# A new order of scores, sums and feed-forward products in the later blocks of an attention and gated-convolution kernel

## The chip, the cores and the metric

The kernel runs on one core of one Trainium2 chip. The metric is the device time of one execution in microseconds (us); before and after are compared by the median of several runs.

## The reference

Attention with a soft cap, and on its output a gated feed-forward layer whose gate is a causal convolution of five taps:

```python
# q, k, v: (8, 12, 448, 64)
scores = (1.0 / np.sqrt(64)) * np.matmul(q, k.transpose(0, 1, 3, 2))
scores = cap * np.tanh(scores / cap)
attn = np.exp(scores - np.max(scores, axis=-1, keepdims=True))
attn = attn / (np.sum(attn, axis=-1, keepdims=True) + 1e-09)
x = np.matmul(attn, v)           # heads side by side: (8, 448, 768)
# xp is x with 4 rows of zeros ahead; conv_w: (5, 768); w_val, w_out: (768, 768)
gate_pre = sum(conv_w[k] * xp[:, k:k + 448, :] for k in range(5))
gate = 1.0 / (1.0 + np.exp(-gate_pre))
out = (gate * (x @ w_val)) @ w_out
```

## The kernel before

The work is cut into 48 head pairs p (8 batches of 6 pairs, two heads side by side on the 128 partitions). For a pair, q and k are loaded in blocks and transposed on VectorE (`tq`, `tk`; lines L296). From pair 13 (`NPLAIN`) on they are split into a high and a low half (`half_hi` on ScalarE, L302, `half_lo` on VectorE, L236) and a score tile is the sum of three products of halves, for both heads: `scores`, L317, tile `pss`, i = 0 to 3 for the four tiles of 112 keys; there are two `pss` buffers. ScalarE makes tanh (L325) and exp (L329) of a tile into `pt`. VectorE adds the four exp tiles of a pair up in `add` (i = 0 and 1: two tiles each, L339; i = 2: the two results, L336). TensorE multiplies them with v (`attnv`, L354, tile `psa`) and with ones (`sums`, L366, tile `psz`). VectorE turns the sums (L374), takes the reciprocal (L380, L381), spreads it (L387) and multiplies (`norm_mul`, L395) into `u`, the pair's 128 columns of x. x is split again: `x_hi` on ScalarE (L400), `x_lo` on VectorE (L236). `conv` has five steps on VectorE (i = 0: L414; 1 to 4: L416), each on top of the one before.

The feed-forward layer of a batch works on its six 128-column blocks. `val` (L437 to L439, tile `psf`) is the product with w_val, 18 matmuls in two parts for a block d; `gate` (L443, VectorE) multiplies it with the sigmoid of the convolution (L422, ScalarE, six of them in one pair of each batch, with a table load), `gated_hi` (L446, ScalarE) and `gated_lo` (L236, VectorE) split the result into `g_h` and `g_l`. `out_part` (L466 to L468, tile `psf`) is the product with w_out, again 18 matmuls, over d = 0 to 5 in this order and so with the block of d = 5 in its last three; `store` (L474, ScalarE) copies it out. There are two `psf` buffers.

No scheduler orders the engines. Each step has a time in units of a pair (`STEADY`, `SPLIT` and other tables for the steps of a pair, `VAL`, `SIG_AT`, `OUT_EVEN` and so on for those of a batch), the steps are sorted by pair + time, and each engine works its instructions off in the order in which they were recorded, waiting on semaphores. So av at 1.10 of pair p stands in the next pair's period, between that pair's scores (0.0, 0.05) and its tanh of tiles 2 and 3. In pairs 13 to 47 the order on TensorE within a period is: scores 0 and 1, `attnv` and `sums` of the pair before, a first feed-forward product, scores 2 and 3, a second one (in two pairs of every second batch two at once). Counted within a batch's six pairs, the feed-forward products lag behind: the pairs with p mod 6 = 1 hold the sigmoids and the value products of d = 1 and 2, p mod 6 = 2 those of d = 3 and 4, p mod 6 = 3 the value product of d = 5 and the first output product, the pairs with 4, 5 and 0 output products, and 0 also the value product of d = 0 of the next batch.

Of the kernel before, what the change touches and what calls it, by code (L numbers as in the profile page):

```python
# [91 lines left out]
    "x_lo": 1.46,  # L92
    "conv": (1.44, 1.54, 1.58, 1.70, 1.74),
}

LATE_X = {"x_lo": 1.76, "conv": (1.78, 1.80, 1.83, 1.86, 1.89)}
NEARLY, NPAIRED, NPLAIN = 6, 11, 13
# [100 lines left out]
def fast_path(tc, io, u2, q, k, v, w_val, conv_w, w_out, out, capt):  # L198
# [8 lines left out]
    NPAIR = H // 2  # L207
    NP = B * NPAIR
# [12 lines left out]
    with ExitStack() as ctx:  # L221
# [77 lines left out]
        def half_hi(name, p):  # L299
            st = state[p]  # L300
            st[name, "h"] = scratch["qk"].tile([P, S], F32R, name=name + "h")
            nc.scalar.copy(st[name, "h"], st[name])  # L302

        def half_lo(name, p):
            st = state[p]
            st[name, "l"] = scratch["qk"].tile([P, S], F32R, name=name + "l")
            less(nc.vector, st[name, "l"], st.pop(name), st[name, "h"])
# [175 lines left out]
        tables = [EARLY if p < NEARLY - 1 else HANDED if p < NEARLY else PAIRED if p < NPAIRED else STEADY if p < NPLAIN else SPLIT for p in range(NP)]  # L483
        for p in range(NPLAIN, NP):
            if p % NPAIR == 0:
                tables[p] = tables[p] | LATE_X

        def at(when, f, *a):
            events.append((when, len(events), f, a))

# [5 lines left out]
            q_hi=lambda p: half_hi("q", p), k_hi=lambda p: half_hi("k", p),  # L496
            q_lo=lambda p: half_lo("q", p), k_lo=lambda p: half_lo("k", p),
            scores=scores, tanh=tanh, exp=exp, add=add, av=attnv, sums=sums, turn_sums=turn_sums, recip=norm_recip,
            spread=spread, mul=norm_mul, x_hi=x_hi, x_lo=x_lo, conv=conv,
        )  # L500
        for p, table in enumerate(tables):
            for name, f in steps.items():
                x = table.get(name, ())
                if isinstance(x, tuple):
                    for i, y in enumerate(x):
                        at(p + y, f, p, i)
                else:
                    at(p + x, f, p)
        for b in range(B):
            t0 = NPAIR * b  # L510
            for d in range(NCC):
                sig = SIG_AT if b else SIG_FIRST
                y = (VAL if b else VAL_FIRST)[d]
                at(t0 + sig, sigmoid, b, d)
                for i in range(PARTS):
                    at(t0 + y + i * PART, val, b, d, i)
                done = t0 + max(y + PARTS * PART, sig + 0.17)
                at(done + 0.01, gate, b, d)

                last = d == NCC - 1  # L520
                at(done + (0.02 if last else 0.08), gated_hi, b, d)
                at(done + (0.03 if last else 0.12), gated_lo, b, d)
            if b % 2 == 0:
                at(t0 + KEEP_AT, keep_tail)
            for m, y in enumerate(OUT_ODD if b % 2 else OUT_LATE if b == B - 2 else OUT_EVEN):
                for i in range(PARTS):
                    at(t0 + y + i * PART / 2, out_part, b, m, i)
                at(t0 + y + 0.20, store, b, m)
                at(t0 + y + 0.40, store_out, b, m)
# [137 lines left out]
def kernel(tc, q, k, v, cap, w_val, conv_w, w_out, out):  # L667
    nc = tc.nc
    with tc.tile_pool(name="cap_pool", bufs=1) as pool, tc.tile_pool(name="io", bufs=2) as io:
        capt = pool.tile([P, 1], F32, name="capt")  # L670
        nc.sync.dma_start(capt, cap.rearrange("(o c) -> o c", o=1).partition_broadcast(P))

        pad = conv_w.shape[0] - 1
        u2 = [pool.tile([P, pad + q.shape[2]], F32, name=f"u{i}") for i in range(2)]
        for t, src in zip(u2, (q, k)):
            load_blocks(nc, t[:, pad:], src, 0)
        mag = pool.tile([1, 1], F32, name="mag")
        nc.vector.scalar_tensor_tensor(mag, capt[0:1], -1.0, capt[0:1], ALU.mult, ALU.max)
        small = pool.tile([1, 1], I32, name="small")
        nc.vector.tensor_scalar(small, mag, CAP_FAST, None, ALU.is_le)  # L680
        flag = nc.values_load(small, min_val=0, max_val=1)
        with tc.If(flag != 0) as cmp:
            fast_path(tc, io, u2, q, k, v, w_val, conv_w, w_out, out, capt)
        with cmp.Else():
            general_path(tc, q, k, v, w_val, conv_w, w_out, out, capt)
# [30 lines left out]
```

## Time and profile before

| | us |
|---|---|
| median of 3 runs | 774.95 |
| lowest, highest | 773.33, 777.27 |
| the profiled execution: its time | 775.05 |
| the profiled execution: span from first to last instruction | 773.3 |
| TensorE (PE) busy | 731.7 |
| VectorE (DVE) busy | 594.9 |
| ScalarE (ACT) busy | 538.8 |

The profiled execution took 775.05, of which 773.3 lie between its first and its last instruction; the rest lies around it. Matmul durations overlap each other, since a matmul starts before the one ahead of it has ended, so the starts are what tells TensorE's pace.

### The profile page before, as it was taken

The numbers are of one execution on the slowest core, as the hardware profiler recorded it, in microseconds if no ns is written. First come the engines' busy times: TensorE is split into PE (matmuls) and PEld (weight loads), VectorE is DVE, ScalarE is ACT, GpSimd is POOL, SyncE is SP. The second block draws the span as 40 slices with busy tenths as digits, with TensorE's granted clock in tenths as the row PEclk, the third lists the DMA queues.
The fourth block names the chain that finished last, engine by engine and source line by source line (L and its number), as shares of the span: only waits on it lengthen the run. The fifth ranks groups of instructions, "written<-read, shape, count | busy, mean of one in ns | idle before, by whom it ended". The sixth has DMA issues, their size and how long they took to land.

```text
span 773.3 us, 10851 instructions
## 1 busy us (share of the span) xinstructions
PE 731.7 (95%) x3972; PEld 490.6 (63%) x3972; DVE 594.9 (77%) x972; ACT 538.8 (70%) x708; POOL 7.8 (1%) x16
## 2 busy tenths in 40 slices
PE   5787899999899999999999999999999999999997
PEld 1232356455676776676766777676666777575997
DVE  2688859878888778998898778998798778997510
ACT  4787677866877669767777669767777669766311
POOL 0000000100000000000000000000000000000000
PEclk9999999999999999999999999999999999999999
DMA  6888745484312333233322333234322333210001
GB/s 117 196 205 216 160 102 133 107 225 98 70 36 52 74 81 57 42 70 83 77 43 47 79 75 62 40 68 85 75 48 47 73 73 71 36 36 31 22 21 65
DMA packets 241820, 63.75 MB, mean 82 GB/s; under 512 B 228448, under 2 KB 235616, under 8 KB 241760
## 3 DMA queue, kind: packets, MB, share of 16 engines
q1 hardware_dynamic: 241760, 62.98, 37.1%
q8 instruction: 33, 0.54, 0.3%
q14 instruction: 27, 0.22, 0.1%
HBM read 51.94 MB, written 11.01 MB: 81 GB/s over the span
## 4 chain that ended last, share of the span: by engine, by line
PE 41%; DVE 20%; ACT 13%; issue 3%; DVEq 0%; ACTq 0%
PE psf L466 7%; PE pss L317 7%; PE psf L467 6%; PE psf L468 6%; PE psa L354 6%; DVE pa L339 4%; ACT pt L325 4%; ACT pt L329 4%; DVE gate L416 3%; PE psf L437 3%; PE psf L438 2%; PE psf L439 2%; ACT gate L422 2%; PE psz L366 2%; DVE g_l L236 1%
## 5 line engine op out<-in xcount | busy, mean ns | idle before, releaser
L325 ACT ACTIVATE pt<-pss,rc 112x896 f32<-112x896 f32 x192 | 186.0, 1005 | 35.4 <-PE pss L317 35.4
L329 ACT ACTIVATE pt<-pt,capt 112x896 f32<-112x896 f32 x192 | 189.2, 1038 | 0.1
L354 PE MATMUL psa<-pt,vn 112*64 112x448 f32 x720 | 147.7, 548 | 0.0
L416 DVE SCALAR_TENSOR_TENSOR gate<-u,cw,gate 128x448 f32<-128x448 f32 x192 | 132.3, 689 | 6.6 <-ACT gate L412 1.1
L466 PE MATMUL psf<-wo,g_h 128*128 128x384 f32 x336 | 117.8, 350 | 0.8 <-DVE wo L142 0.8
L437 PE MATMUL psf<-xh,wv 128*128 128x448 f32 x288 | 110.1, 382 | 5.8 <-DVE gate L443 3.1
L467 PE MATMUL psf<-wo,g_h 128*128 128x384 f32 x336 | 113.1, 337 | 1.1 <-DVE wo L146 1.1
L468 PE MATMUL psf<-wo,g_l 128*128 128x384 f32 x336 | 113.2, 337 | 0.0
L438 PE MATMUL psf<-xh,wv 128*128 128x448 f32 x288 | 105.3, 365 | 0.0
L439 PE MATMUL psf<-xl,wv 128*128 128x448 f32 x288 | 105.2, 365 | 0.0
L339 DVE TENSOR_TENSOR pa<-pt 112x896 f32<-112x896 f32 x84 | 91.1, 1084 | 16.1 <-ACT pt L329 16.1
L354 PEld LDWEIGHTS psa<-pt,vn 112*64 112x64 f32 x720 | 47.5, 137 | 82.3 <-issue 73.3
L400 ACT CAST xh<-u 128x448 fp32r<-128x448 f32 x48 | 27.1, 565 | 86.8 <-DVE u L395 86.8
L466 PEld LDWEIGHTS psf<-wo,g_h 128*128 128x128 f32 x336 | 63.5, 189 | 23.1 <-issue 17.8
L437 PEld LDWEIGHTS psf<-xh,wv 128*128 128x128 f32 x288 | 54.5, 189 | 34.0 <-issue 20.9
L374 DVE STREAM_TRANSPOSE zt<-psz 128x448 f32<-128x448 f32 x45 | 29.0, 644 | 60.2 <-PE psz L366 60.1
L317 PE MATMUL pss<-qt,kt 64*112 64x448 f32 x208 | 53.2, 630 | 22.8 <-ACT pt L325 14.2
L467 PEld LDWEIGHTS psf<-wo,g_h 128*128 128x128 f32 x336 | 63.6, 189 | 1.4 <-DVE wo L146 1.4
L468 PEld LDWEIGHTS psf<-wo,g_l 128*128 128x128 f32 x336 | 63.5, 189 | 0.3
L446 ACT CAST g_h<-gate 128x448 fp32r<-128x448 f32 x48 | 26.3, 562 | 48.5 <-DVE gate L443 48.3
L474 ACT COPY osb<-psf 128x384 f32<-128x384 f32 x56 | 26.8, 479 | 45.9 <-PE psf L468 45.9
L317 PE MATMUL pss<-qh,kh 64*112 64x448 f32 x280 | 58.5, 412 | 0.0
(74 smaller groups left out, 904.5 us busy)
## 6 DMA issues: line engine op xcount, KB each, us to landing
vn<-in_v_dram SPq DMA_DIRECT2D x96, 112.0 KB, 2.6
out_dram<-osb SPq DMA_DIRECT2D x56, 192.0 KB, 1.9
qn<-in_q_dram SPq DMA_DIRECT2D x188, 56.0 KB, 2.5
kn<-in_k_dram SPq DMA_DIRECT2D x188, 56.0 KB, 2.4
w_raw<-in_moe_w_val_dram SPq DMA_DIRECT2D x12, 384.0 KB, 4.6
w_late<-in_moe_w_val_dram SPq DMA_DIRECT2D x12, 384.0 KB, 5.1
w_raw<-in_moe_w_out_dram SPq DMA_DIRECT2D x12, 384.0 KB, 3.8
w_late<-in_moe_w_out_dram SPq DMA_DIRECT2D x12, 384.0 KB, 4.4
```

The source lines that it names most:

```text
L317: nc.tensor.matmul(ps[:CH, j, :S], st[x][r, c], st[y][r], start=(n == 0), stop=(n == len(parts) - 1))
L325: nc.scalar.activation(st["p", i], st.pop(("s", i)), AF.Tanh, scale=rc8[:CH])
L329: nc.scalar.activation(t, t, AF.Exp, scale=capt[:CH])
L339: nc.vector.tensor_tensor(st["a", i], st["p", 2 * i], st["p", 2 * i + 1], op=ALU.add)
L354: nc.tensor.matmul(st["o"][r, :S], vloads[p][:, j, i], t[:, j], start=(i == 0), stop=(i == NKT - 1))
L416: nc.vector.scalar_tensor_tensor(g, u[:, i:i + S], cw[:, hp, i:i + 1], g, ALU.mult, ALU.add)
L437: nc.tensor.matmul(o, w_h, xh, start=(c == 0), stop=False)
L438: nc.tensor.matmul(o, w_l, xh, start=False, stop=False)
L439: nc.tensor.matmul(o, w_h, xl, start=False, stop=(c == NCC - 1))
L466: nc.tensor.matmul(o, g_h[:, d, s], w_h, start=(d == 0), stop=False)
L467: nc.tensor.matmul(o, g_h[:, d, s], w_l, start=False, stop=False)
L468: nc.tensor.matmul(o, g_l[:, d, s], w_h, start=False, stop=(d == NCC - 1))
```

## The change

Three new tables are laid over the tables of pairs 14 to 47, except those with p mod 6 = 1, which hold the sigmoids (`together`). In such a pair (`TOGETHER`) scores 2 and 3 move from 0.62 and 0.67 to 0.31 and 0.32, right behind the `sums` of the pair before (0.28) and ahead of the first feed-forward product (0.36); their tanh and exp move up as well, and all three adds are done in the pair itself (0.52, 0.60, 0.61) and not in the next (1.03, 1.06). `NEXT_TOGETHER`, for the pair ahead of such a pair, moves the end of that pair's work, which falls in the next period: convolution steps 1 to 4 go from 1.61 to 1.70 to 2.16 to 2.19, two periods on. `PREPARE_TOGETHER` moves the low halves of q and k of the pair behind such a pair. The work itself, its tiles and its buffers stay as they are.

```diff
--- before.py
+++ after.py
@@ -93,6 +93,19 @@
     "conv": (1.44, 1.54, 1.58, 1.70, 1.74),
 }
 
+
+TOGETHER = {
+    "scores": (0.0, 0.05, 0.31, 0.32),
+    "tanh": (0.06, 0.13, 0.34, 0.36),
+    "exp": (0.22, 0.29, 0.47, 0.53),
+    "add": (0.52, 0.60, 0.61),
+}
+NEXT_TOGETHER = {
+    "turn_sums": 1.41, "recip": 1.42, "spread": 1.43, "mul": 1.44, "x_hi": 1.45, "x_lo": 1.54,
+    "conv": (1.58, 2.16, 2.17, 2.18, 2.19),
+}
+PREPARE_TOGETHER = {"q_hi": -0.69, "k_hi": -0.68, "q_lo": -0.44, "k_lo": -0.43}
+
 LATE_X = {"x_lo": 1.76, "conv": (1.78, 1.80, 1.83, 1.86, 1.89)}
 NEARLY, NPAIRED, NPLAIN = 6, 11, 13
 
@@ -484,6 +497,17 @@
         for p in range(NPLAIN, NP):
             if p % NPAIR == 0:
                 tables[p] = tables[p] | LATE_X
+
+        def together(p):
+            return NPLAIN < p < NP and p % NPAIR != 1
+
+        for p in range(NPLAIN, NP):
+            if together(p - 1):
+                tables[p] = tables[p] | PREPARE_TOGETHER
+            if together(p):
+                tables[p] = tables[p] | TOGETHER
+            if together(p + 1):
+                tables[p] = tables[p] | NEXT_TOGETHER
 
         def at(when, f, *a):
             events.append((when, len(events), f, a))
```

On TensorE, where pair 27 (p mod 6 = 3) has the end of the value product of d = 5 (L437 to L439; psf, xh, xl are its result and the halves of x) and the start of the first output product (L466 to L468; g_h and g_l are the halves of the gated blocks), there stands before:

```order
1086 L437 MATMUL psf<-xh,wv 128x448
1087 L438 MATMUL psf<-xh,wv 128x448
1088 L439 MATMUL psf<-xl,wv 128x448
1089 L317 MATMUL pss<-qh,kh 112x448 x2
1090 L317 MATMUL pss<-ql,kh 112x448 x2
1091 L317 MATMUL pss<-qh,kl 112x448 x2
1092 L317 MATMUL pss<-qh,kh 112x448 x2
1093 L317 MATMUL pss<-ql,kh 112x448 x2
1094 L317 MATMUL pss<-qh,kl 112x448 x2
1095 L466 MATMUL psf<-wo,g_h 128x384
1096 L467 MATMUL psf<-wo,g_h 128x384
1097 L468 MATMUL psf<-wo,g_l 128x384
```

The six rows with pss, scores 2 and 3, lie between the two products. After the change the lines have other numbers (317 is now 330, 437 to 439 are 450 to 452, 466 to 468 are 479 to 481), and the same place, from the end of the value product on, with the waits, is:

```order
1392 L451 MATMUL psf<-xh,wv 128x448
1393 L452 MATMUL psf<-xl,wv 128x448
1394 L479 MATMUL psf<-wo,g_h 128x384 [waits DVE_49,Pool_49]
...
1407 L480 MATMUL psf<-wo,g_h 128x384
1408 L481 MATMUL psf<-wo,g_l 128x384 [waits DVE_49]
1409 L479 MATMUL psf<-wo,g_h 128x384 [waits Activation_49]
1410 L480 MATMUL psf<-wo,g_h 128x384
1411 L481 MATMUL psf<-wo,g_l 128x384 [waits DVE_49]
1412 L330 MATMUL pss<-qh,kh 112x448 [waits PE_49]
```

The output product now follows the value product directly; its last three matmuls, those of d = 5, wait for ScalarE's g_h and VectorE's g_l, and the scores of pair 28 stand behind them.

On VectorE, in the same pair, from the multiplication into u (L395) on, there stands before (pa are the sums of exp tiles, L339 and L336):

```order
477 L395 TENSOR_TENSOR u_63<-psa,zt 128x448
478 L339 TENSOR_TENSOR pa_3742<-pt 112x896
479 L236 TENSOR_TENSOR ql<-qt,qh 128x448
480 L236 TENSOR_TENSOR kl<-kt,kh 128x448
481 L236 TENSOR_TENSOR xl<-u_63,xh 128x448
482 L414 TENSOR_SCALAR gate<-u_63,cw 128x448
483 L416 SCALAR_TENSOR_TENSOR gate<-u_63,cw,gate 128x448
484 L443 TENSOR_TENSOR gate<-psf,gate 128x448
485 L416 SCALAR_TENSOR_TENSOR gate<-u_63,cw,gate 128x448
486 L236 TENSOR_TENSOR g_l<-gate,g_h 128x448
487 L416 SCALAR_TENSOR_TENSOR gate<-u_63,cw,gate 128x448 x2
488 L339 TENSOR_TENSOR pa_3806<-pt 112x896
```

The gate of d = 5 (L443) and its g_l stand between the convolution steps, ahead of the second add. After the change, from the four convolution steps that have come into this period up to the same gate and g_l:

```order
465 L429 SCALAR_TENSOR_TENSOR gate<-u_64,cw,gate 128x448 x4
466 L387 STREAM_TRANSPOSE zt<-psz 128x448
...
470 L408 TENSOR_TENSOR u_63<-psa,zt 128x448
471 L352 TENSOR_TENSOR pa_3761<-pt 112x896
472 L249 TENSOR_TENSOR xl<-u_63,xh 128x448
473 L249 TENSOR_TENSOR ql<-qt,qh 128x448
474 L249 TENSOR_TENSOR kl<-kt,kh 128x448
475 L427 TENSOR_SCALAR gate<-u_63,cw 128x448
476 L352 TENSOR_TENSOR pa_3771<-pt 112x896
477 L349 TENSOR_TENSOR pa_3761<-pa_3761,pa_3771 112x896
478 L456 TENSOR_TENSOR gate<-psf,gate 128x448
479 L249 TENSOR_TENSOR g_l<-gate,g_h 128x448
```

The gate has come to stand behind both adds (L352 with pa_3771 and L349), and four convolution steps of the pair before stand ahead of the turn of the sums (L387).

## Rows read from the trace of the kernel before

**Rows 1.** The page: span, busy times, and the group of convolution steps 1 to 4.

```profile
span 773.3 us, 10851 instructions
PE 731.7 (95%) x3972; PEld 490.6 (63%) x3972; DVE 594.9 (77%) x972; ACT 538.8 (70%) x708; POOL 7.8 (1%) x16
...
L416 DVE SCALAR_TENSOR_TENSOR gate<-u,cw,gate 128x448 f32<-128x448 f32 x192 | 132.3, 689 | 6.6 <-ACT gate L412 1.1
```

**Rows 2.** Timeline of TensorE, pair 29: start, duration, what.

```profile
436.85 0.46 PE L317 MATMUL pss<-qh,kh 64*112 64x448 f32 x2
...
438.26 0.60 PE L354 MATMUL psa<-pt,vn 112*64 112x448 f32 x2
...
441.32 0.92 PE L366 MATMUL psz<-pa,ones 112*64 112x448 f32 x4
442.17 0.45 PE L466 MATMUL psf<-wo,g_h 128*128 128x384 f32 x1
...
445.23 0.34 PE L468 MATMUL psf<-wo,g_l 128*128 128x384 f32 x1
445.50 0.46 PE L317 MATMUL pss<-qh,kh 64*112 64x448 f32 x2
...
446.91 0.44 PE L466 MATMUL psf<-wo,g_h 128*128 128x384 f32 x1
...
453.38 0.46 PE L317 MATMUL pss<-qh,kh 64*112 64x448 f32 x2
```

**Rows 3.** Timeline of TensorE, pair 27 and the start of pair 28.

```profile
405.96 0.46 PE L317 MATMUL pss<-qh,kh 64*112 64x448 f32 x2
...
414.79 0.37 PE L439 MATMUL psf<-xl,wv 128*128 128x448 f32 x1
...
416.50 0.44 PE L466 MATMUL psf<-wo,g_h 128*128 128x384 f32 x1
...
419.58 0.34 PE L468 MATMUL psf<-wo,g_l 128*128 128x384 f32 x1
419.85 0.46 PE L317 MATMUL pss<-qh,kh 64*112 64x448 f32 x2
```

**Rows 4.** Timeline of ScalarE: pair 27, and tanh 0 of pair 29.

```profile
418.19 0.57 ACT L446 CAST g_h<-gate 128x448 fp32r<-128x448 f32 x1 [3.60 <-DVE gate L443]
418.66 1.90 ACT L325 ACTIVATE pt<-pss,rc 112x896 f32<-112x896 f32 x2
...
437.76 1.01 ACT L325 ACTIVATE pt<-pss,rc 112x896 f32<-112x896 f32 x1 [0.32 <-PE pss L317]
```

**Rows 5.** Timeline of TensorE, last pair: v products and sums of pair 47.

```profile
709.30 3.23 PE L354 MATMUL psa<-pt,vn 112*64 112x448 f32 x16
714.24 0.97 PE L366 MATMUL psz<-pa,ones 112*64 112x448 f32 x4 [1.72 <-DVE pa L336]
```

**Rows 6.** Timeline of VectorE, pair 27 and the start of pair 28.

```profile
411.39 0.65 DVE L374 STREAM_TRANSPOSE zt<-psz 128x448 f32<-128x448 f32 x1
...
413.85 1.08 DVE L339 TENSOR_TENSOR pa<-pt 112x896 f32<-112x896 f32 x1
...
416.45 0.45 DVE L414 TENSOR_SCALAR gate<-u,cw 128x448 f32<-128x448 f32 x1
...
417.54 0.62 DVE L443 TENSOR_TENSOR gate<-psf,gate 128x448 f32<-128x448 f32 x1
...
418.79 0.63 DVE L236 TENSOR_TENSOR g_l<-gate,g_h 128x448 fp32r<-128x448 f32 x1
...
422.45 1.09 DVE L339 TENSOR_TENSOR pa<-pt 112x896 f32<-112x896 f32 x1 [1.72 <-ACT pt L329]
423.58 1.09 DVE L336 TENSOR_TENSOR pa<-pa,pa 112x896 f32<-112x896 f32 x1
```

**Rows 7.** Windows: stretch, busy time of each engine (instructions), granted TensorE clock, DMA.

```profile
209.00:215.00 6.00, 4.01 (x15) 3.38 (x12) 5.73 (x10) 4.51 (x6) 0.00 (x0) 0.72 0.08 13
712.00:717.00 5.00, 3.28 (x19) 2.08 (x16) 3.71 (x6) 0.00 (x0) 0.00 (x0) 1.00 0.12 43
```

## The prediction

> **What bounds the kernel now.** I read the page first. The reader is to see that TensorE is busy for 95% of the span, VectorE for 77%, ScalarE for 70% [rows 1]. A busy share says little about slack, so I went on to the timeline of TensorE and walked one head pair after another, each from its first score matmul to that of the next pair (pairs 0 to 47; pair 27 begins at 405.96, pair 29 at 436.85).
>
> Pair 29 shows what a pair costs when nothing waits [rows 2]: two score tiles 1.41 us (436.85 to 438.26), the products with v of the pair before 3.06, its sums 0.85, one output product 3.33, two more score tiles 1.41, then two output products 6.47: 16.53 together. Within a product the 18 matmuls start 0.18 apart (442.17 to 445.23 is 17 steps); from its last matmul to a score it is 0.27. So TensorE runs without a gap, and a change can win only the seams between kinds of work and the few waits left.
>
> The waits: pair 28 has the same work as pair 29 and took 17.00 (419.85 to 436.85), 0.47 more [rows 2, 3]. ScalarE shows why: a cast of a gated block waited 3.60 for VectorE and stood ahead of tanh 2 and 3 of pair 27, which began at 418.66 [rows 4]; everything behind them, the adds on VectorE included, came late, and the sums of pair 27 with them. The other wait is at the end: from the first v product of pair 47 to its sums it is 4.94 (709.30 to 714.24) where pair 29 has 3.06, so 1.88 of waiting for the adds [rows 2, 5].
>
> **What the change removes.** Scores 2 and 3 go behind the sums, so the seam "product, then score" in the middle of a pair turns into "product, then product". That is 0.27 against 0.18, 0.09 saved; I take the same where one product is of w_val. Sums to score I price like sums to product. Of the 34 pairs from 14 on, 29 have the new table, and pair 47 had no first product to be moved past: 28 x 0.09 = 2.6 us. [...]
>
> The 0.47 of each pair that follows the first output product (16, 22, 28, 34, 40, 46) goes, since tanh 2 and 3 now stand far ahead of that cast and both adds are done in the pair itself: 6 x 0.47 = 2.8. For pair 47 I walked VectorE: its two adds can run once exp 3 is done, before its sums are due, so 1.9 goes as well. Pairs 13, 19, 25, ... with sigmoids keep their tables and so does the wait behind them. Gains together 7.3; the seams could give nothing and the tail nothing, so 2.8 to 7.3.
>
> The four late convolution steps of a pair move into the next one, behind the transposes of q and k, where in most pairs VectorE would wait for the sums anyway. ScalarE does the same work in another order and stays below TensorE. DMAs stand in the same order on SP's queue. None of these is on the path, but for one place.
>
> **What it adds.** That place is the pair with the last value product of a block and its first output product (15, 21, 27, 33, 39, 45). The output product needs, for its last three matmuls, the sixth gated block: the value product, then VectorE's gate, ScalarE's cast to g_h, VectorE's g_l. Before, scores 2 and 3 lay between the two products and the gate stood early on VectorE: gate at 417.54, cast 418.19, g_l 418.79 to 419.42 [rows 4, 6]; the last three matmuls of a product that ran from 416.50 to 419.58 came just in time [rows 3]. Now there is nothing between the products, and the gate stands on VectorE behind both adds.
>
> I count from the start of pair 27. TensorE reaches scores 2 and 3 at 1.41 + 3.06 + 0.85 = 5.32 and the value product at 6.73. That one took 13.89 (405.96 to 419.85) - 5.32 - 1.41 - 3.35 (416.50 to 419.85) = 3.81 with a seam of 0.30 (414.79 to 415.09 is where scores follow it) that falls to 0.2, so 3.7 [rows 3]. The output product starts at 10.45, its sixteenth matmul would be due at 13.15, the next pair at 13.80.
>
> VectorE cannot begin to turn the sums before they are there, 4.47 + 0.92 = 5.4 [rows 2]. Its queue ahead of that holds the fifth gate, a transpose, the fifth g_l, a transpose and four convolution steps. That g_l needs a cast on ScalarE, behind tanh 0, which starts 0.91 after its pair (437.76 against 436.85) and takes 1.0 [rows 4]: cast to 2.4, g_l to 3.05, transpose to 3.6, four steps of 0.69 [rows 1] and a little each to 6.35. From the turn to the end of the first convolution step it is the same set of instructions as at 411.39 to 416.90, 5.5 us; the two adds are 422.45 to 424.67, 2.2; the gate 0.62 [rows 6]. The gate ends at 14.6, the cast (0.57) at 15.2, g_l (0.63) at 15.8. The sixteenth matmul waits from 13.15 to 15.2, the eighteenth until 15.8, and the next pair starts near 16.05 instead of 13.80: 2.25 lost. TensorE's queue holds the next pair's scores behind those matmuls, so nothing hides it. Six times is 13.5. If VectorE's queue were free at 5.4 the loss would be 1.3 each, 7.8 in all; half a us more on VectorE makes it 2.75 and 16.5.
>
> **The clock.** One thing about such a hole is not decided by the sum. From 209 to 215 TensorE was busy for 4.01 of 6.00 us, so idle for 1.99, and was granted 0.72 of its clock, part of it at 1.2 GHz; from 712 to 717 it was idle for 1.72 and kept 1.00 [rows 7]. A fall costs (1 - 0.72) x 6.00 = 1.7 us. The new holes are about 1.8, between these two. I take one fall in six.
>
> Sum: the profiled execution took 775.05 with 1.75 around the span, and the median is 774.95, so I start from 775.0. 775.0 - 7.3 + 13.5 = 781.2, and 1.7 for one fall: **782.9 us**.
>
> **Rivals.**
> (a) The holes are there and the clock falls after nearly each: 781.2 + 6 x 1.7 = 791.4. For it: 1.99 was enough once. Against it: 1.72 was not. The Trainium skill says on the page "TensorE: Matmul & The Clock Gate", section "The HAM clock gate", that the throttled clock is the default and that activity releases it; by that, each hole puts the clock at risk.
> (b) The short hole: the fifth cast comes early and VectorE is not late for the sums. 775.0 - 7.3 + 7.8 = 775.5, no change to be seen.
> (c) No hole, faster: the sixth gate is done by the time the sixteenth matmul is due, so that only the gains are left, 775.0 - 7.3 = 767.7. This needs VectorE to end that gate 2.05 earlier than I have it, which is the two adds' worth (2.2); the order of VectorE speaks against it, since the adds stand ahead of the gate, and the turn of the sums cannot start before 5.4, from where even a punctual chain ends at 13.7 for the gate and 14.3 for the cast. It decides from 1.2 us of hole (7.3 / 6) downwards.
> (d) The gains don't come, the holes do: 775.0 - 2.8 + 13.5 + 1.7 = 787.4.
>
> **How the numbers follow.** Forecast, holes of about 2.2 with none to three falls of the clock, and (d) with it: 0.62, between 780 and 788. (a): 0.16. (b): 0.10. (c): 0.12. What this kernel's measurement can tell from no change is about 0.5%, 3.9 us. Slower takes the forecast and (a), 0.78; same is (b), 0.10; faster is (c), 0.12. The range leaves out (c) and the far end of (a): 775 to 790.
>
> **What would show it.** In the trace of the changed kernel the first output product of a block shows a hole of about 2 us ahead of its sixteenth matmul, ended by the cast on ScalarE, six times; pair 27 takes about 16 us instead of 13.89; pair 28 about 16.4 instead of 17.00; the sums of pair 47 no longer wait; the granted clock falls after some of the holes. The prediction is wrong if the sixth gate ends before the output product reaches it, if VectorE runs the chain from sums to adds in less than 8 us, or if a pair without that place gets longer, which would mean a wait that I have not seen.

## The result and the profile after

| | before | after |
|---|---|---|
| median, us | 773.33 (7 runs, 770.61 to 777.27) | 780.65 (7 runs, 778.10 to 781.76) |
| ratio, 95% interval | | 1.0090 [1.0062, 1.0117] |
| pair 27, us | 13.89 | 16.06 |
| pair 28, us | 17.00 | 16.29 |
| pair 29, us | 16.53 | 16.32 |
| from the start of pair 14 to the end of the span, us | 556.65 | 562.89 |

The kernel became 0.9% slower, as predicted. The profiled execution took 778.10 with a span of 776.2, only 2.9 more than the span of before [rows 1]. Ahead of pair 14, where the change moves nothing, that one execution was 3.3 us quicker (pair 14 starts at 213.31, before at 216.65; 1.6 of it is pair 13, where the clock had fallen in before and not in after). From pair 14 on it is 6.24 slower, so I read stretches from there.

The page of after: span, busy times, and two groups (line, engine, operation, tiles, shape, count | busy, mean ns | idle before, its releaser).

```profile
span 776.2 us, 10855 instructions
PE 725.0 (93%) x3972; PEld 492.1 (63%) x3972; DVE 591.9 (76%) x972; ACT 537.3 (69%) x708; POOL 6.7 (1%) x16
...
L479 PE MATMUL psf<-wo,g_h 128*128 128x384 f32 x336 | 115.8, 345 | 12.3 <-ACT g_h L459 10.9
...
L459 ACT CAST g_h<-gate 128x448 fp32r<-128x448 f32 x48 | 26.3, 562 | 55.3 <-DVE gate L456 55.2
```

TensorE has no more work than before, but its output products now wait 10.9 us for ScalarE's cast `g_h`, and that cast waits for VectorE's gate. The timeline of TensorE in pair 27 shows where (it answers to [rows 3]).

```profile
405.59 0.46 PE L330 MATMUL pss<-qh,kh 64*112 64x448 f32 x2
...
416.04 0.34 PE L479 MATMUL psf<-wo,g_h 128*128 128x384 f32 x1
...
418.48 0.34 PE L481 MATMUL psf<-wo,g_l 128*128 128x384 f32 x1
420.63 0.45 PE L479 MATMUL psf<-wo,g_h 128*128 128x384 f32 x1 [1.81 <-ACT g_h L459]
420.91 0.34 PE L480 MATMUL psf<-wo,g_h 128*128 128x384 f32 x1
421.29 0.44 PE L481 MATMUL psf<-wo,g_l 128*128 128x384 f32 x1
421.65 0.46 PE L330 MATMUL pss<-qh,kh 64*112 64x448 f32 x2
```

Fifteen matmuls of the first output product run in step, then TensorE stands idle for 1.81 us ahead of the sixteenth. Such a row stands six times in the trace, in pairs 15, 21, 27, 33, 39 and 45, each with 1.81 or 1.82. VectorE in the same pair (answering to [rows 6]):

```profile
409.09 2.81 DVE L429 SCALAR_TENSOR_TENSOR gate<-u,cw,gate 128x448 f32<-128x448 f32 x4
411.82 0.64 DVE L387 STREAM_TRANSPOSE zt<-psz 128x448 f32<-128x448 f32 x1
...
417.23 1.09 DVE L352 TENSOR_TENSOR pa<-pt 112x896 f32<-112x896 f32 x1
418.35 1.09 DVE L349 TENSOR_TENSOR pa<-pa,pa 112x896 f32<-112x896 f32 x1
419.36 0.62 DVE L456 TENSOR_TENSOR gate<-psf,gate 128x448 f32<-128x448 f32 x1
420.61 0.62 DVE L249 TENSOR_TENSOR g_l<-gate,g_h 128x448 fp32r<-128x448 f32 x1 [0.63 <-ACT g_h L459]
```

The trace marks no idle time of VectorE from the four convolution steps to the end of the gate: the gate is late because of what stands ahead of it, not because of its product, which had ended before 416.3. ScalarE's row in that pair closes the chain: it had been idle for 3.13 us when the gate came (answering to [rows 4]).

```profile
420.01 0.56 ACT L459 CAST g_h<-gate 128x448 fp32r<-128x448 f32 x1 [3.13 <-DVE gate L456]
```

At the end of the kernel the sums of pair 47 follow their products in 3.06 us (714.53 to 717.59) where before took 4.94 [rows 5]:

```profile
714.53 3.23 PE L367 MATMUL psa<-pt,vn 112*64 112x448 f32 x16
717.59 0.92 PE L379 MATMUL psz<-pa,ones 112*64 112x448 f32 x4
```

The clock, by windows of after (columns as in [rows 7]): behind the holes of pairs 15 and 33, behind the hole of pair 27, and around an idle time of 1.99 in pair 13.

```profile
243.00:249.00 6.00, 5.96 (x28) 3.08 (x29) 3.81 (x7) 4.08 (x5) 0.00 (x0) 0.72 0.09 33
512.50:518.50 6.00, 5.96 (x28) 2.98 (x29) 3.85 (x7) 4.15 (x5) 0.99 (x2) 0.72 0.09 33
421.00:427.00 6.00, 5.96 (x37) 2.54 (x35) 3.94 (x7) 4.91 (x7) 0.00 (x0) 1.00 0.09 34
206.50:212.50 6.00, 4.01 (x25) 3.36 (x22) 5.63 (x11) 4.52 (x7) 0.00 (x0) 1.00 0.17 28
```

The granted clock fell to half (1.2 of 2.4 GHz) for 3.41 us behind two of the six holes, and kept 1.00 behind the other four. The count of matmuls that fall into the six microseconds tells the price: 28 at 0.72, 37 at 1.00.

### The profile page after: what moved, and what is told of

Read it like the earlier page. It is cut to its first block, busy times and chain, and to the rows that moved or that the text cites. A ratio compares the mean times of both kernels' runs of the same rounds, so it can differ in the third digit from the quotient of the medians.

```text
span 776.2 us, 10855 instructions
## 1 busy us (share of the span) xinstructions
PE 725.0 (93%) x3972; PEld 492.1 (63%) x3972; DVE 591.9 (76%) x972; ACT 537.3 (69%) x708; POOL 6.7 (1%) x16
## 4 chain that ended last, share of the span: by engine, by line
PE 52%; DVE 14%; ACT 10%; issue 1%; DVEq 0%; ACTq 0%
PE pss L330 10%; PE psa L367 8%; PE psf L479 7%; PE psf L481 7%; PE psf L480 6%; PE psf L450 4%; DVE gate L429 4%; PE psf L451 4%; PE psf L452 4%; ACT pt L338 3%; PE psz L379 3%; DVE pa L352 2%; ACT gate L435 2%; DVE pa L349 2%; ACT pt L342 1%
## 5 line engine op out<-in xcount | busy, mean ns | idle before, releaser
L429 DVE SCALAR_TENSOR_TENSOR gate<-u,cw,gate 128x448 f32<-128x448 f32 x192 | 130.1, 678 | 5.1
L479 PE MATMUL psf<-wo,g_h 128*128 128x384 f32 x336 | 115.8, 345 | 12.3 <-ACT g_h L459 10.9
L480 PE MATMUL psf<-wo,g_h 128*128 128x384 f32 x336 | 112.4, 335 | 1.1 <-DVE wo L159 1.1
L450 PE MATMUL psf<-xh,wv 128*128 128x448 f32 x288 | 107.8, 374 | 4.2 <-DVE gate L456 3.1
L451 PE MATMUL psf<-xh,wv 128*128 128x448 f32 x288 | 104.4, 363 | 0.0
L352 DVE TENSOR_TENSOR pa<-pt 112x896 f32<-112x896 f32 x84 | 91.1, 1084 | 4.9 <-ACT pt L342 4.9
L387 DVE STREAM_TRANSPOSE zt<-psz 128x448 f32<-128x448 f32 x45 | 28.9, 642 | 72.5 <-PE psz L379 72.4
L330 PE MATMUL pss<-qt,kt 64*112 64x448 f32 x208 | 50.6, 601 | 24.9 <-ACT pt L338 16.2
L452 PEld LDWEIGHTS psf<-xl,wv 128*128 128x128 f32 x288 | 54.0, 187 | 3.7
```

The lines of the kernel that those rows point to most:

```text
L330: nc.tensor.matmul(ps[:CH, j, :S], st[x][r, c], st[y][r], start=(n == 0), stop=(n == len(parts) - 1))
L352: nc.vector.tensor_tensor(st["a", i], st["p", 2 * i], st["p", 2 * i + 1], op=ALU.add)
L429: nc.vector.scalar_tensor_tensor(g, u[:, i:i + S], cw[:, hp, i:i + 1], g, ALU.mult, ALU.add)
L450: nc.tensor.matmul(o, w_h, xh, start=(c == 0), stop=False)
L451: nc.tensor.matmul(o, w_l, xh, start=False, stop=False)
L452: nc.tensor.matmul(o, w_h, xl, start=False, stop=(c == NCC - 1))
```

## The experiments

The theory: the sixth gate stands on VectorE behind both adds of the pair and behind four convolution steps that an earlier pair hands over (in pair 27 those of pair 25), so that the cast `g_h` comes too late for the sixteenth matmul of the first output product. The rivals: the loss is not in the order of VectorE, but in the two products standing side by side (the value product's result or the buffers are late anyway); or it comes from the clock alone; or the earlier scores load ScalarE so that everything behind them slips.

Seven kernels ran. The column "from pair 14" is the stretch from the first score of pair 14 to the end of the span, less the 556.65 of before, good to 0.1; "falls" counts, of the six places, those with a fall of the clock right behind.

| run | median (before beside it) | ratio, 95% interval | pair 27 | idle there | from pair 14 | falls |
|---|---|---|---|---|---|---|
| after | 780.65 (773.33) | 1.0090 [1.0062, 1.0117] | 16.06 | 1.81 | +6.2 | 2 |
| without p mod 6 = 3 | 770.54 (773.91) | 0.9968 [0.9949, 0.9988] | 14.68 | 0.20 | -1.7 | 0 |
| gate ahead of both adds | 761.01 (773.91) | 0.9846 [0.9823, 0.9870] | 13.67 | none | -11.5 | 0 |
| p mod 6 = 3 alone | 778.55 (773.91) | 1.0069 [1.0046, 1.0092] | 15.39 | 1.13 | +5.7 | 0 |
| one add more ahead | 792.26 (773.91) | 1.0246 [1.0224, 1.0268] | 17.20 | 2.94 | +20.3 | 6 |
| gate between the adds | 770.60 (772.67) | 0.9972 [0.9955, 0.9989] | 14.94 | 0.68 | -3.4 | 0 |
| gate first, later steps | 761.23 (772.67) | 0.9841 [0.9822, 0.9860] | 14.16 | 0.21 | -10.9 | 0 |
| scores alone | 768.79 (772.67) | 0.9942 [0.9924, 0.9961] | 14.04 | none | -4.4 | 0 |

### The pairs with the hole left as they were

```diff
-            return NPLAIN < p < NP and p % NPAIR != 1
+            return NPLAIN < p < NP and p % NPAIR not in (1, 3)
```

> The pairs with the last value product and the first output product of a batch (p mod 6 = 3) are taken out of the new tables; the other 23 keep them. My theory (the loss sits in the hole ahead of the sixteenth matmul of that output product): no hole, pair 27 back to about 13.9 us, the 0.47 us wait of pair 28 back, seams of 0.2 us saved in 22 pairs and the wait at the end gone: before - 4.4 - 1.9, about 767. Rival (the loss is spread over the new order, the merged products or VectorE's order in all pairs): still slower than before, 778 or more.

It took 770.54, 0.3% less than before and some 3.5 us more than I had expected. The hole is gone, but pair 27 is not back at 13.89. The timeline of TensorE in that pair:

```profile
412.98 0.44 PE L479 MATMUL psf<-wo,g_h 128*128 128x384 f32 x1
...
415.54 0.34 PE L481 MATMUL psf<-wo,g_l 128*128 128x384 f32 x1
416.08 0.44 PE L479 MATMUL psf<-wo,g_h 128*128 128x384 f32 x1 [0.20 <-ACT g_h L459]
...
417.11 0.46 PE L330 MATMUL pss<-qh,kh 64*112 64x448 f32 x2
```

Even with scores 2 and 3 between the products the sixteenth matmul waits for the cast. The four convolution steps that pair 25 still hands over stand ahead of the turn of the sums on VectorE and make the gate late: the turn starts 6.23 after the pair (402.43), as in after, where before has 5.43, and pair 27 is 0.79 longer than before, six times 4.7 us. VectorE there:

```profile
405.94 2.81 DVE L429 SCALAR_TENSOR_TENSOR gate<-u,cw,gate 128x448 f32<-128x448 f32 x4
408.66 0.65 DVE L387 STREAM_TRANSPOSE zt<-psz 128x448 f32<-128x448 f32 x1
```

Pair 28 took 16.98, so its old wait is back too. The removal of the hole is as the theory has it; that these pairs would return to their old length was wrong.

### The gate and its halves ahead of both adds

`d` is the block, `last` is d = 5, `done` is the time of the value product's end in the table, and t0 + 9 is the pair in whose period it lies.

```diff
-                at(done + 0.01, gate, b, d)
...
-                at(done + (0.02 if last else 0.08), gated_hi, b, d)
-                at(done + (0.03 if last else 0.12), gated_lo, b, d)
+                when = (-0.055, -0.035, -0.03) if last and together(t0 + 9) else (0.01, 0.02, 0.03) if last else (0.01, 0.08, 0.12)
+                for y, f in zip(when, (gate, gated_hi, gated_lo)):
+                    at(done + y, f, b, d)
```

> All new tables stay, TensorE's order is that of the change; on VectorE the gate of d = 5 and its g_l go ahead of both adds (gate behind q_lo, g_l behind the first convolution step), in the six pairs with p mod 6 = 3. My theory (the gate queued behind the adds makes the hole): gate ends about 11.5 us after the pair's start, cast 12.1, g_l 13.0, all before TensorE needs them at 13.15 and 13.5; no hole, no fall of the clock in these pairs, pair 27 about 13.7 us; before - 28 x 0.2 - 2.8 - 1.9 = about 763. Rival (with nothing between the two products the gate chain is too long whatever VectorE's order): a hole of 1 us or more stays, 769 or more.

It took 761.01, within 2 us of what the theory expected. The two products still stand side by side, all three tables are in force, and only VectorE's and ScalarE's order around one gate differs. TensorE, then VectorE, in pair 27 (from 399.87 to 413.54, so 13.67):

```profile
410.32 0.34 PE L479 MATMUL psf<-wo,g_h 128*128 128x384 f32 x1
...
413.27 0.34 PE L481 MATMUL psf<-wo,g_l 128*128 128x384 f32 x1
413.54 0.46 PE L330 MATMUL pss<-qh,kh 64*112 64x448 f32 x2
```

```profile
410.61 0.62 DVE L456 TENSOR_TENSOR gate<-psf,gate 128x448 f32<-128x448 f32 x1
...
412.04 0.62 DVE L249 TENSOR_TENSOR g_l<-gate,g_h 128x448 fp32r<-128x448 f32 x1
412.57 1.08 DVE L352 TENSOR_TENSOR pa<-pt 112x896 f32<-112x896 f32 x1
413.69 1.09 DVE L349 TENSOR_TENSOR pa<-pa,pa 112x896 f32<-112x896 f32 x1
```

The gate starts 10.74 after its pair instead of 13.77, the 18 matmuls of the output product start within 2.95 without a gap, and the adds that now end at 414.78 are in nobody's way: pair 28 took 16.31. So neither the neighbourhood of the products nor the load of ScalarE made the loss. This is the fastest order tried (one below is level with it), better than before and after.

### Only the pairs with the hole

```diff
-            return NPLAIN < p < NP and p % NPAIR != 1
+            return NPLAIN < p < NP and p % NPAIR == 3
```

> Only the six pairs with p mod 6 = 3 get the new tables. My theory: the holes come alone, without most of the gains: 6 x about 2.1 us, one to three falls of the clock at 1.7, less 6 x 0.47 of waits in the pair behind: 783 to 788, slower than the whole change. Rival (the loss is spread over all pairs): within 3 us of before.

Slower than before, but at 778.55 by less than expected. The six holes are there and shorter, and no fall of the clock follows them. TensorE ahead of the sixteenth matmul of pair 27 (402.31 to 417.70), then VectorE's turn of the sums:

```profile
416.66 0.44 PE L479 MATMUL psf<-wo,g_h 128*128 128x384 f32 x1 [1.13 <-ACT g_h L459]
```

```profile
407.75 0.65 DVE L387 STREAM_TRANSPOSE zt<-psz 128x448 f32<-128x448 f32 x1
...
415.40 0.62 DVE L456 TENSOR_TENSOR gate<-psf,gate 128x448 f32<-128x448 f32 x1
```

The turn starts 5.44 after its pair, not 6.23 as in after, since pair 25 keeps its table and hands over no convolution steps. So the pair loses 1.50 and not 2.17: without those four steps each hole is about 0.7 shorter. The adds weigh more, since with the gate ahead of them no hole is left even with the steps in place. I had expected the whole hole of after; that was my oversight. It also answers the rival of the clock: no fall stands behind these holes, and the kernel is slower than before all the same.

### One add more ahead of the gate

The second add of the pair is computed a second time, with the same result, between the adds and the gate.

```diff
+                st["again"] = other
+                return
+            if i == 3:
+                nc.vector.tensor_tensor(st.pop("again"), st["p", 2], st["p", 3], op=ALU.add)
...
+                if last and together(t0 + 9):
+                    at(done, add, t0 + 9, 3)
```

> The whole change, and VectorE does the second add of exp tiles once more (same result) between the adds and the gate of d = 5 in the six pairs: one operation of 1.0 us ahead of the gate. My theory: each hole grows by about 1.0 us, idle 2.8 instead of 1.8, pair 27 about 17.1 us: 6 us more than the change, 786.7; and the clock falls after most of the holes, not two of six, up to 7 us more, 794. Rival on the clock (falls there are chance, not the length of the hole): still two or fewer falls, 786 to 787. Rival (no hole on the path): no slower than the change.

It took 792.26, inside what was expected if the clock falls behind nearly all holes. TensorE and VectorE (the repeated add, L353) in pair 27, and windows behind the holes of pairs 27 and 33:

```profile
425.51 0.45 PE L483 MATMUL psf<-wo,g_h 128*128 128x384 f32 x1 [2.94 <-ACT g_h L463]
```

```profile
423.23 1.09 DVE L353 TENSOR_TENSOR pa<-pt 112x896 f32<-112x896 f32 x1
```

```profile
426.30:432.30 6.00, 6.00 (x29) 3.03 (x31) 3.52 (x6) 4.66 (x6) 0.00 (x0) 0.72 0.09 33
519.30:525.30 6.00, 5.76 (x21) 3.21 (x23) 4.33 (x7) 3.53 (x6) 1.36 (x2) 0.50 0.09 33
```

One add of 1.09 makes the idle time 1.13 longer: what stands ahead of the gate goes straight into TensorE's wait. The clock fell behind all six, for 3.41 us four times and for 6.83 twice. From pair 14 on this kernel is 14.1 slower than after; the six pairs with the hole account for 7.4 of it (1.14 in pair 27), and the rest lies in the pairs behind them, where the clock fell (pair 28 took 17.87, not 16.29).

### The gate between the two adds

```diff
-                when = (-0.055, -0.035, -0.03) if last and together(t0 + 9) else (0.01, 0.02, 0.03) if last else (0.01, 0.08, 0.12)
+                when = (-0.015, -0.014, -0.012) if last and together(t0 + 9) else (0.01, 0.02, 0.03) if last else (0.01, 0.08, 0.12)
```

(This diff is against the kernel with the gate ahead of both adds.)

> The whole change, with the gate of d = 5 and its g_l between the two adds on VectorE in the six pairs, so one add of 1.0 us earlier, not two. My theory: the hole shrinks by about 1.0 us and breaks in two short waits, pair 27 about 15.1 us instead of 16.06, and with idle stretches of about 1 us the clock no longer falls there: the change's 780.7 - 6 - 3 = 771 to 772. Rival (the length of the wait is set by ScalarE's cast or the value product, not by the adds): 780.

```profile
416.32 0.44 PE L479 MATMUL psf<-wo,g_h 128*128 128x384 f32 x1 [0.68 <-ACT g_h L459]
```

It took 770.60, as expected but for the wait, which is a single one of 0.68. The idle time goes down by 1.13 with one add out of the way, as it went up by 1.13 with one more. Pair 27 with two adds and a repetition, two, and one ahead of the gate takes 17.20, 16.06 and 14.94; with none 13.67, where TensorE itself is the limit.

### Gate first, and the last convolution steps later

In after and in the fastest order a wait is left in pairs 20, 26, 32, 38 and 44, whose sums come 0.8 behind the last product with v instead of 0.37. On top of the gate-first order, convolution steps 3 and 4 of the pairs with p mod 6 = 0 move here behind the adds that these sums wait for.

```diff
-LATE_X = {"x_lo": 1.76, "conv": (1.78, 1.80, 1.83, 1.86, 1.89)}
+LATE_X = {"x_lo": 1.76, "conv": (1.78, 1.80, 1.83, 2.065, 2.07)}
```

> The version with the gate and its g_l ahead of both adds, and with the last two convolution steps of pairs with p mod 6 = 0 moved behind the adds of the pair after them, where in five pairs (20, 26, 32, 38, 44) the sums still wait 0.4 us for those adds. Theory: that wait goes, 5 x 0.4 = 2 us below the version without it, 759. Rival: ScalarE's exp of the pair with the sigmoids sets those adds, not VectorE's queue, and nothing changes, 761.

761.23, no different from 761.01. The wait is gone, pair 26 took 14.15 instead of 14.66, but pair 27 took 14.16 instead of 13.67. TensorE and VectorE there:

```profile
412.72 0.44 PE L481 MATMUL psf<-wo,g_l 128*128 128x384 f32 x1 [0.21 <-DVE g_l L249]
```

```profile
412.05 0.62 DVE L249 TENSOR_TENSOR g_l<-gate,g_h 128x448 fp32r<-128x448 f32 x1
```

VectorE's g_l starts 13.12 after TensorE began the pair (398.93), in the other kernel 12.17 (399.87 to 412.04): TensorE reaches the pair earlier, VectorE does not. It is idle for 0.63 us only from 397.11 to 414.79, and the two moved steps still stand ahead of the gate, so the wait moves. Less work on VectorE there was not tried, so that its queue is full there is read from the trace and not shown by a run.

### Only the scores moved

`TOGETHER` is cut to its scores, the other two tables are empty, so VectorE and ScalarE keep the order of before.

```diff
+TOGETHER = {"scores": (0.0, 0.05, 0.31, 0.32)}
+NEXT_TOGETHER = {}
+PREPARE_TOGETHER = {}
```

> TensorE's part alone: scores 2 and 3 move as in the change, ScalarE and VectorE keep the order of before, so the gate of d = 5 stays early among the convolution steps. My theory: no hole of 1.8 us in pair 27 (gate ends about 12.2 us after the pair's start, cast 12.8, g_l 13.45), seams saved in 28 pairs, but tanh 2 and 3 stay behind the casts and copies, so the wait ahead of the sums in pair 28 stays or grows by some tenths: 767 to 770, faster than before. Rival (the two products being neighbours makes the hole, whatever the vector order): holes of 1 us or more in the six pairs, 775 or more.

768.79, as expected. Pair 27 took 14.04; no idle time is marked in its output product, but the last matmul starts 0.38 behind the one ahead of it, when g_l has ended (414.92). The end of that product, and the sums of pair 47, which wait as before:

```profile
414.59 0.34 PE L472 MATMUL psf<-wo,g_h 128*128 128x384 f32 x1
414.97 0.44 PE L473 MATMUL psf<-wo,g_l 128*128 128x384 f32 x1
...
707.35 0.97 PE L371 MATMUL psz<-pa,ones 112*64 112x448 f32 x4 [1.72 <-DVE pa L341]
```

Pair 28 took 16.76: its sums still come late. So the moved scores by themselves bring the seams, 4.4 us net from pair 14 on; it is the order on VectorE and ScalarE that removes the waits, and that of VectorE that makes the hole.

## Why the prediction was right

**The place and the chain.** Counted from the start of pair 27, us:

| | predicted | measured |
|---|---|---|
| turn of the sums starts | 6.35 | 6.23 |
| output product starts | 10.45 | 10.45 |
| gate of d = 5 ends | 14.6 | 14.39 |
| sixteenth matmul starts | 15.2 | 15.04 |
| g_l ends | 15.8 | 15.64 |
| next pair starts | 16.05 | 16.06 |

The runs with one add more and one less ahead of the gate show that the adds set the end of this chain, and the run with those pairs alone shows what the convolution steps add. It also measured what I had bounded: with VectorE free when the sums come (5.4), I had a loss of 1.3 against 13.80, so the next pair at 15.1; with the turn at 5.44 it started at 15.39.

**The holes.** My 2.25 was counted against 13.80, a pair with its seam already saved; against the 13.89 of before it is 2.16, 13.0 for six. Four of the six pairs took 2.17 or 2.18 more, 13.05 at that rate. The six together took 96.80 instead of 83.34, 13.5 more: in the other two (pairs 15 and 33, 16.32 and 16.22) the clock fell before the pair had ended, which holds the other 0.4.

**The gains** came to 9.4, where I had 7.3, 6.8 of it outside the six pairs with the hole. Three parts: the last pair's wait (1.9, as predicted); the six pairs behind the hole, 0.67 to 0.72 each without falls of the clock, of which 0.47 is the wait that I had, and 0.2 the seam, 4.1 together; and 16 other pairs, 3.4. The mis-sized term is the seam, "0.27 against 0.18, 0.09 saved": pair 29 shows 0.21. The timeline of TensorE in pair 29, first the start of the second output product before, then the two products of after behind the scores:

```profile
446.91 0.44 PE L466 MATMUL psf<-wo,g_h 128*128 128x384 f32 x1
447.19 0.33 PE L467 MATMUL psf<-wo,g_h 128*128 128x384 f32 x1
```

```profile
444.68 0.44 PE L479 MATMUL psf<-wo,g_h 128*128 128x384 f32 x1
444.96 0.33 PE L480 MATMUL psf<-wo,g_h 128*128 128x384 f32 x1
445.13 0.34 PE L481 MATMUL psf<-wo,g_l 128*128 128x384 f32 x1
...
447.76 0.33 PE L481 MATMUL psf<-wo,g_l 128*128 128x384 f32 x1
447.93 0.33 PE L479 MATMUL psf<-wo,g_h 128*128 128x384 f32 x1
448.10 0.33 PE L480 MATMUL psf<-wo,g_h 128*128 128x384 f32 x1
```

Behind the scores the second matmul starts 0.28 after the first, and only the third 0.17 after it; behind another product all follow in 0.17. So a switch costs 0.1 at the first start and 0.1 more at the second, and I had counted the first alone. In the 22 pairs without the hole that is 22 x 0.09 = 2.0 predicted and 22 x 0.21 = 4.6 measured. (28 x 0.09 is 2.5 and not 2.6, and no run bears out that the seams could give nothing.) The Trainium skill, page "TensorE: Matmul & The Clock Gate", section "Back-to-back issue gap", gives the spacing of an isolated matmul by its columns alone, from which 162.5 ns is an estimate for 384 columns. It has no price for a switch, and the trace shows 0.17 to 0.18 within a product and both delays at a switch.

**The clock.** I took one fall in six at 1.7; the profiled execution has two, which made pair 16 17.54 instead of the 16.32 of the order with the gate first, and pair 34 14.52 instead of 13.20, 2.5 together. With the 0.4 in pairs 15 and 33 a fall cost 1.5. Rival (a) is what one more add brings, not this change.

**The sum.** 13.5 + 2.5 - 9.4 = 6.6, and the trace from pair 14 on has 6.24; the other 0.4 lies behind the last matmul, which starts 5.4 ahead of the end of the span before and 5.0 after, for a reason that stays open. The medians differ by 7.3, and I had 7.9. That the two are so close is in part luck: gains that were too small by 2.6 stood against a clock that was too cheap by 1.2. The profiled execution was the quickest of the seven and had a mean granted clock of 0.989; the other six had 0.981 to 0.984. That points to more falls in them, but how many stood behind the holes was not seen. Of the rivals, (b) and (c) needed VectorE early at the turn or at the gate, and it was at neither; (d) is refuted by the pairs without the hole: those with sigmoids kept their time, pairs 16 and 34 got longer behind a fall of the clock, and all others got shorter. So the sign "a pair without that place gets longer" did come, by the clock and not by a new wait.

## What to carry to other kernels

When two products that depend on each other are put side by side, look for the engine that makes the second one's input out of the first one's result, and read what stands in its queue ahead of that step: here two adds that nobody needed yet cost TensorE 1.1 and 1.3 us, and moving one gate ahead of them turned 0.9% slower into 1.5% faster. Each change of order should be followed to the engine that waits, pair by pair, since a mean over the span (TensorE 93% busy instead of 95%) tells only that something waits. And a wait taken away from one period may come back in the next if the engine behind it is full there, as the run with later convolution steps showed.

## What the hardware showed that I had not expected

In pair 29 a switch between score tiles and an output product delays two starts and not one: 0.27 at the first score behind a product, and 0.28 at the second matmul of a product behind scores, where 0.17 is the pace within a product.

The clock's falls go with the length of the idle time, but length alone does not decide. In the first output products (one profiled execution of each kernel) no fall followed idle times of 0.68 (six) and 1.03 to 1.14 (six), two followed the six of 1.81, and all six of 2.94 were followed by one. An idle time of 1.99 stands in pair 13 of every trace; a fall followed it before, with one add more, and with only the scores moved, and not in the other runs, in after for instance (the last of the windows above). Earlier in the kernel longer ones show both outcomes too: 2.30 to 2.35 near 153 us had a fall in four of the nine traces, and 2.79 near 90 us in the run with later convolution steps had none. The Trainium skill, page "TensorE: Matmul & The Clock Gate", section "The HAM clock gate", has the throttled clock as the default that activity releases; the runs agree in direction, since falls stand behind idle times of 1.81 and more. What decides at one length between the two outcomes stays open.
